# Two placement rules in a weight arena: how many places early gate loads must leave, and where output blocks go

## The chip, the cores and the metric

The kernel runs on one core of one Trainium2 chip. The time is that of the device for one launch, in microseconds, and lower is better. TensorE (PE) multiplies, VectorE (DVE), ScalarE (ACT) and GpSimd (POOL) do the rest, and every large transfer is issued from the queue of SyncE (SP).

## The reference

Eight sequences of 448 positions pass through an attention block of 12 heads (head size 64) with normalized queries and keys, and then through a gated feed-forward layer:

```python
q_n, k_n = rmsnorm(q, g_q), rmsnorm(k, g_k)
scores = scale * np.matmul(q_n, k_n.transpose(0, 1, 3, 2))
attn = exp(scores - max) / (sum + 1e-09)
x = np.matmul(attn, v)                 # then (B,H,S,D) -> (B*S, H*D) = (3584, 768)
xn = x / rms(x) * rms_g
g, val = xn @ w_gate, xn @ w_val       # 768 x 1536 each
out = (g * sigmoid(g) * val) @ w_out   # 1536 x 768
```

All data are float32 for the engines.

## The kernel before, in words

**Staging.** Attention runs over pairs of heads, six pairs to a sequence. While the pairs of sequence b + 1 are computed, the feed-forward work of sequence b is filled in between their blocks. `fill` (from L1630) takes the next feed-forward item from a list, calls it through `pe`, and afterwards lets other engines' work be issued. `pe` counts steps: `now["t"]` is the planner's clock, and everything that is to be issued "n steps later" (`after`) is put down by it. The order of instructions on every engine is thus fixed by this Python code, and engines run their instructions in that order.

**Gate and value of the second sequence (b = 1).** From the second sequence on, the two products with `w_gate` and `w_val` are made together, with a scheme of 15 products of thirds and halves of the matrices (`PRODUCTS`) in place of 18. It runs over four groups of three 128-wide column blocks, in the order 0, 2, 1, 3 (`GROUPS`), called here the first to the fourth. One product is eight matmuls of 224 columns (L1182). Its weight operand is either one of nine raw blocks (`b11` to `b33`) or one of nine sums of two or three raw blocks (`v9`, `v4`, `v5`, `v7`, `v1`, `v14`, `v11`, `v10`, `v13`, in the order of their use). The left operands are sums too, made once per sequence. What leaves PSUM is added up on VectorE (L1200, L1203, L1255) or copied by ScalarE (L1197), and a finished column block becomes `h` through L1214 and L1215.

For the second sequence alone the weight sums do not exist yet. Each is made by `derive` on VectorE: a first `tensor_tensor` of 128x512 at L1087, a second at L1090, or only one of them. It is put five steps later into a scratch tensor in HBM (`kept`, L1095), from where later sequences load it ready-made. `derive` makes the sums strictly in order, only from raw blocks whose loads were asked for five or more steps ago, and only if a place is free. `fill` calls it once a step at the third and fourth step after a block of attention has begun, and later than that up to about two instructions a step. If a product is due whose sum is missing, the sum is made at once.

**Places.** All weight blocks lie in an arena of 66 units of 128 columns (`places`, `block`, `give_back`). A gate block takes 4 units, aligned to 4 (kind `wg`; `wg1` adds six spare places outside the arena); an output block takes 3 units, counted from the upper end (kind `w`). While sums of the output weights for the third sequence are still to be made (`todo_q` is not empty), the upper 18 units are set apart (kind `side`), which leaves 48 units: 12 + 6 places for gate blocks, or 16 for output blocks, in the same units. `block` takes the place that has been free longest. A block of the second sequence is given back three steps after its last use, others one step after.

**Loads.** `ask` (L1038) runs whenever a place comes free. It goes through one list of uses: the nine raw blocks of each of the four groups, then the 42 output blocks of the second sequence, then the third sequence's gate blocks, and so on. A load is issued (L1066) only if `keep_free` places would still be free after it: 6 for the second sequence's gate blocks, 3 for others, 1 for the first seven of the third sequence. Output blocks wait until all 36 weight sums are made. Blocks for the side sums (`wd`, `wx`, L1046) go into the side zone.

**Output sums.** `derive_o` (L1122) makes sums of output-weight blocks for the second sequence, and only in steps in which `derive` made none. `derive_q` (L1150 to L1153) makes those for the third sequence, in 21 jobs of four instructions. It needs two free gate places, and it is held back while one of the third sequence's first seven gate loads is the next to be asked for. The output products of the second sequence are at L1447 and those of the third at L1518.

Of the kernel before, what the change touches and what calls it, by code (L numbers as in the profile page):

```python
# [335 lines left out]
def safe_scores(  # L336
# [40 lines left out]
    now, due = {"t": 0}, []  # L377
# [146 lines left out]
    def norm_k(g, half):  # L524

        if g >= NG:
            return
        for n in range(NK * half, NK * (half + 1)):
            block = st["qk", g][:, 1, n * D:(n + 1) * D]
            nc.scalar.activation(block, block, ACT.Copy, scale=st["rs", g][:, 2 * NK + n:2 * NK + n + 1])  # L530
# [248 lines left out]
    def hurry(jobs):  # L779
        while jobs:  # L780
# [12 lines left out]
    RIGHT_G = {"v9": ("b11", "b33", None), "v4": ("b21", None, "b32"), "v5": ("b12", None, "b23"),  # L793
               "v1": ("b21", "b33", "b31"), "v14": ("b12", "b21", "b22"), "v11": ("b22", "b23", "b32"),
               "v10": ("b13", "b12", "-b33"), "v13": ("b13", "b11", "b23"), "v7": ("b31", "b11", "-b32")}
# [41 lines left out]
    freed = {i: 0 for i in range(UNITS)}  # L837
# [11 lines left out]
    def zone():  # L849

        return 18 if todo_q else 0

    def places(kind):

        lim = UNITS - (zone() if count["done"] else 0)
        if kind[0:2] == "wg":
            spans = [range(i, i + 4) for i in range(0, lim - 3, 4)]
            if kind == "wg1":
                spans += [range(i, i + 4) for i in sorted(spare) if i % 4 == 0]
        elif kind == "side":  # L860
            spans = [range(i, i + 3) for i in range(lim, UNITS, 3)]
        else:
            spans = [range(i - 3, i) for i in range(lim, 2, -3)]
        return [span for span in spans if None not in [freed[i] for i in span]]

    def block(kind="w"):
        span = min(places(kind), key=lambda span: (max(freed[i] for i in span), span[0]))
        for i in span:
            freed[i] = None
        if span[0] in spare:  # L870
            return spare[span[0]], span
        return arena[:, span[0] * 128:span[-1] * 128 + 128], span

    def room(many, kind="w"):
        return len(places(kind)) >= many
# [11 lines left out]
    def data(key):  # L887
        return st[key][0][:, 0:GW if key[0] == "wg" else BW]
# [40 lines left out]
    turn_of, count = {"n": 0}, {"done": False, "cv": 0}  # L929
# [8 lines left out]
    def home(key):  # L938
        if key[0] == "w":
            g, j = divmod(key[2], KG)  # L940
            at = 2 * key[4] + key[3]
            return kept[g, j:9:3, :, at * 128:(at + 1) * 128].rearrange("k p n -> p k n")
        if key[0] == "wg":
            return kept[key[2], NAMES_G.index(key[3])]
        if key[0] == "wq":
            n = min(2, PARTS_Q - 2 * key[3]) * HW
            return kept_q[key[2]][:, 2 * HW * key[3]:2 * HW * key[3] + n]
        return kept_o[NAMES.index(key[2]), key[3]]
# [5 lines left out]
    def convert():  # L954
# [5 lines left out]
        if 0 <= n - 5 < len(pieces):  # L960
            key = pieces[n - 5][0]
            st[key] = block()
            lo, top = st.pop(("cv", n - 5))
            nc.gpsimd.tensor_tensor(data(key).bitcast(I32), top, lo, ALU.add)
# [61 lines left out]
    asked = {"n": 0, "derived": 0}  # L1026
# [4 lines left out]
    derived = [(g, to) for g in GROUPS for _, _, to in PRODUCTS if to in RIGHT_G]  # L1031
# [6 lines left out]
    def ask():  # L1038

        if turn_of["n"] < TURNS:  # L1040
            return
        while side and (room(1, "side") or side[0][0] == "wd" and asked["derived"] > 32 and room(4, "wg")):
            key = side.pop(0)
            asked[key] = now["t"]
            st[key] = block("side" if room(1, "side") else "wg")
            nc.sync.dma_start(out=data(key), in_=home(key))  # L1046
        while asked["n"] < len(uses):
            key = uses[asked["n"]]
            kind, keep_free = "wg" if key[0] == "wg" else "w", 3
            if key[1] == 1 and key[0] == "wg":  # L1050
                kind, keep_free = "wg1", 6
            elif asked["derived"] < len(derived):
                return
            elif asked["n"] in next_gate:
                keep_free = 1
            if key[0] == "wo" and key[2][0] == "T" and ("kept", *key[2:]) not in asked:
                return
            if key[0] == "wq" and asked.get("sums_q", 0) < KG * (key[2] + 1):
                return
            if not room(keep_free + 1, kind):  # L1060
                return
            asked["n"] += 1
            asked[key] = now["t"]
            st[key] = block(kind)
            src = home(key)
            nc.sync.dma_start(out=data(key)[:, 0:src.shape[-1]], in_=src)  # L1066
# [66 lines left out]
    todo_q = list(jobs_q)  # L1133
# [34 lines left out]
    def used(key):  # L1168
        give_back(key)
        after(3 if key[0:2] == ("wg", 1) else 1, ask)  # L1170
# [459 lines left out]
    def fill(n=None):  # L1630
# [8 lines left out]
        for _ in range(min(n, len(todo))):  # L1639
# [5 lines left out]
            while asked["derived"] < made or (key and key not in st):  # L1645
                before = dict(asked)
                derive(0)
                if key and key[0] == "wo":
                    derive_o(0)
                ask()  # L1650
                if before == asked:
                    pe(idle)
# [263 lines left out]
```

## Time and profile before

| what | us |
|---|---|
| three runs: lowest, median, highest | 1530.95, 1531.31, 1538.87 |
| the profiled execution, its own time | 1533.21 |
| the profiled execution, first to last instruction (span) | 1531.4 |
| TensorE busy in the span | 1484.1 |
| VectorE, GpSimd, ScalarE busy | 1039.9, 738.6, 604.0 |

A row of the groups or of a timeline names the engine, the line of the code, the operation, the tile written and the tiles read, and how often it ran; a bracket at its end gives the idle time just before it and what ended it. "raw", "top" and "top_x" are names of spare tiles that serve as weight places or left operands; "w" is the arena. A row of the waits names the waiting instruction and the one that it waited for, with the total, the count and the longest. A row of the stretches gives, after the stretch and its length, the busy time of each engine, the clock granted to TensorE (1.00 is full), the busy share of the DMA engines and GB/s. The second sequence's gate and value stage lies between 285 and about 424 us of the span, its output stage from there to 490, and the third sequence's two stages from 490 to about 680.

### The profile page before, as it was taken

Reading aid. Unit: us, or ns where it says so; the run is one execution under the profiler, and the core shown is the slowest. Engines: PE = TensorE matmul, PEld = TensorE weight load, DVE = VectorE, ACT = ScalarE, POOL = GpSimd, SP = SyncE. Lnnn points to the kernel's source line nnn. Section 1 sums busy time; section 2 is a strip of 40 time slices with the busy share of each in tenths; the row PEclk is TensorE's granted clock in tenths of the full one; section 3 lists DMA queues with packets and bytes.
Section 4 is the critical chain, followed back from the end, with each engine's and each line's share of the span. In section 5 each row is a group of like instructions: output and inputs, shape, how many; then the busy total and the mean of one; then the engine's idle time right before and its main releaser. Section 6 shows DMA issues by size and latency. Waiting matters only on the chain.

```text
span 1531.4 us, 25718 instructions
## 1 busy us (share of the span) xinstructions
PE 1484.1 (97%) x8732; PEld 1155.8 (75%) x8732; DVE 1039.9 (68%) x1826; ACT 604.0 (39%) x1377; POOL 738.6 (48%) x708
## 2 busy tenths in 40 slices
PE   8999999998999999899999999999999999999997
PEld 4344445687755888787988788759788789899996
DVE  5777999687855687874568655635668655674664
ACT  6856765344322443224442443334542443201100
POOL 6967987555433453364544644345644632021002
PEclk9999999999999999999999999999999999999998
DMA  7758675775577899885557865576457755597675
GB/s 190 224 164 237 183 237 169 231 250 187 188 235 231 283 309 317 285 254 191 174 152 237 247 186 160 162 228 190 133 162 246 223 157 145 154 301 227 167 237 170
DMA packets 302176, 322.51 MB, mean 211 GB/s; under 512 B 81620, under 2 KB 243668, under 8 KB 302036
## 3 DMA queue, kind: packets, MB, share of 16 engines
q1 hardware_dynamic: 301108, 320.58, 68.8%
q8 instruction: 72, 1.18, 0.3%
q14 instruction: 68, 0.56, 0.1%
q10 hardware_dynamic: 800, 0.20, 0.1%
q0 software_dynamic: 128, 0.00, 0.0%
HBM read 266.90 MB, written 53.77 MB: 209 GB/s over the span
## 4 chain that ended last, share of the span: by engine, by line
PE 83%; DVE 10%; DMA 2%; issue 2%; SPq 1%; ACT 1%; POOL 1%; DVEq 0%; POOLq 0%; ACTq 0%
PE ff L1182 37%; PE ff L1518 12%; PE sc L659 8%; PE av L674 7%; PE ff L1589 6%; PE ff L1447 5%; PE tr L545 2%; PE ff L1320 1%; PE den L692 1%; DVE l L1392 1%; PE den L607 1%; PE sc L563 1%; DMA vt<-in_v_dram 1%; PE av L590 1%; DVE ms L496 1%
## 5 line engine op out<-in xcount | busy, mean ns | idle before, releaser
L714 POOL TENSOR_TENSOR es<-es,e 128x448 f32<-128x448 f32 x205 | 252.2, 1230 | 13.6
L1182 PE MATMUL ff<-x,w 128*128 128x224 f32 x1272 | 254.0, 353 | 1.4 <-DVE pb L1203 1.1
L1182 PEld LDWEIGHTS ff<-x,w 128*128 128x128 f32 x1272 | 238.5, 190 | 4.2 <-DVE pb L1203 1.4
L659 PE MATMUL sc<-qT,kT 64*64 64x448 f32 x1176 | 232.7, 541 | 5.6 <-DVE x L744 3.9
L674 PE MATMUL av<-e,vt 64*64 64x448 f32 x984 | 193.3, 538 | 0.0
L664 ACT ACTIVATE e<-sc 128x448 f32<-128x448 f32 x294 | 155.0, 547 | 80.9 <-PE sc L659 59.4
L1182 PE MATMUL ff<-xs,w 128*128 128x224 f32 x848 | 168.4, 353 | 2.6 <-DVE w L1087 1.3
L1182 PEld LDWEIGHTS ff<-xs,w 128*128 128x128 f32 x848 | 158.6, 190 | 6.3 <-issue 3.4
L644 POOL TENSOR_TENSOR ss<-ss,rd 128x448 f32<-128x448 f32 x40 | 46.8, 1170 | 210.3 <-ACT rd L643 210.3
L659 PEld LDWEIGHTS sc<-qT,kT 64*64 64x64 f32 x1176 | 78.8, 133 | 88.2 <-issue 59.9
L709 POOL TENSOR_TENSOR es<-e 128x448 f32<-128x448 f32 x41 | 47.3, 1154 | 192.5 <-ACT e L664 192.5
L1518 PE MATMUL ff<-w,l 128*128 128x192 f32 x630 | 119.1, 331 | 6.8 <-DVE pb L1552 3.0
L1203 DVE TENSOR_TENSOR pc<-ff,l 128x448 f32<-128x448 f32 x56 | 34.9, 623 | 122.9 <-PE ff L1182 91.7
L515 POOL TENSOR_TENSOR rs<-ms,mhalf 128x12 f32<-128x12 f32 (+1 forms) x50 | 115.3, 2307 | 4.2
L1518 PEld LDWEIGHTS ff<-w,l 128*128 128x128 f32 x630 | 104.2, 191 | 13.8 <-DVE pb L1552 4.2
L1589 PE MATMUL ff<-x,w 128*128 128x448 f32 x288 | 111.8, 541 | 0.0
L674 PEld LDWEIGHTS av<-e,vt 64*64 64x64 f32 x984 | 66.0, 133 | 41.3 <-issue 41.3
L1200 DVE TENSOR_TENSOR pb<-ff,pb 128x448 f32<-128x448 f32 x84 | 52.4, 623 | 63.0 <-PE ff L1182 53.5
L1589 PEld LDWEIGHTS ff<-x,w 128*128 128x128 f32 x288 | 53.3, 190 | 51.1 <-issue 47.6
L1182 PE MATMUL ff<-top_x,w 128*128 128x224 f32 x424 | 89.4, 361 | 2.1 <-DVE w L1090 2.1
L1182 PEld LDWEIGHTS ff<-top_x,w 128*128 128x128 f32 x424 | 80.2, 193 | 13.4 <-issue 10.2
L1489 POOL TENSOR_TENSOR y<-y,pa 128x384 f32<-128x384 f32 x10 | 11.3, 1154 | 157.4 <-DVE y L1564 144.4
(210 smaller groups left out, 2892.2 us busy)
## 6 DMA issues: line engine op xcount, KB each, us to landing
w<-kept SPq DMA_DIRECT2D x383, 256.0 KB, 3.4
w<-kept_q SPq DMA_DIRECT2D x350, 192.0 KB, 3.8
w<-kept_o SPq DMA_DIRECT2D x150, 192.0 KB, 4.0
kept_q<-w SPq DMA_DIRECT2D x63, 192.0 KB, 3.4
qk<-in_q_dram SPq DMA_DIRECT2D x48, 192.0 KB, 3.8
qk<-in_k_dram SPq DMA_DIRECT2D x96, 96.0 KB, 3.8
raw<-in_moe_w_gate_dram SPq DMA_DIRECT2D x24, 384.0 KB, 4.5
raw<-in_moe_w_val_dram SPq DMA_DIRECT2D x24, 384.0 KB, 4.3
```

Source lines behind the costliest of these rows:

```text
L515: nc.gpsimd.tensor_tensor(st["rs", g][:, cols], ms, mhalf[:, cols], ALU.pow)
L644: after(m, lambda: (nc.gpsimd.tensor_tensor(ss, ss, rd, ALU.add), st.update({("summed", b): hp})))
L659: nc.tensor.matmul(ps[r, 0:S], lhsT=st["kT", g][r, keys_of(i)], rhs=st["qT", g][r, :], start=True, stop=True)
L664: nc.scalar.activation(e, ps[:, 0:S], ACT.Exp)
L674: nc.tensor.matmul(st["av", g][own(j), 0:S], lhsT=vt, rhs=st["e", g, i][r], start=i == 0, stop=i == PARTS - 1, skip_group_check=True)
L709: nc.gpsimd.tensor_tensor(st["es", g], st["e", g, 0], st["e", g, 1], ALU.add)
L714: nc.gpsimd.tensor_tensor(st["es", g], st["es", g], st["e", g, i], ALU.add)
L1182: nc.tensor.matmul(bank[:, w * HT:(w + 1) * HT], lhsT=data(key)[:, (2 * w + c) * 128:(2 * w + c + 1) * 128], rhs=a[left][:, c, :], start=o ...
L1200: nc.vector.tensor_tensor(T[name], ps[:, 0:S], T[name], ALU.add)
L1447: nc.tensor.matmul(ps, lhsT=left_o(b, which, LEFT_O[name], c), rhs=data(("wo", b, name, c)), start=first and c == 0, stop=c == NFP - 1, sk ...
L1518: nc.tensor.matmul(ps, lhsT=a[:, j, :], rhs=data(key)[:, n % 2 * HW:(n % 2 + 1) * HW], start=start and j == 0, stop=j == KG - 1, skip_grou ...
L1589: nc.tensor.matmul(bank[w][:, 0:S], lhsT=data(key)[:, c * 128:(c + 1) * 128], rhs=st["x", 0][:, 3 * half + c, :], start=half == c == 0, st ...
```

## The change

It touches two functions. In `ask`, the raw gate blocks of the second sequence must leave six places free only until the first group's nine sums are made; from then on four are enough. In `block`, an output block that is placed while the side zone exists takes, among the places that have been out of use for at least two steps, the highest one, and otherwise the longest-free one, the highest first; it used to take the place that was free longest, the lowest first.

```diff
     def block(kind="w"):
-        span = min(places(kind), key=lambda span: (max(freed[i] for i in span), span[0]))
+        last = lambda span: max(freed[i] for i in span)
+        order = lambda span: (last(span), span[0])
+        if kind == "w" and count["done"] and todo_q:
+            order = lambda span: (max(last(span), now["t"] - 2), -span[0])
+        span = min(places(kind), key=order)
@@ in ask()
             if key[1] == 1 and key[0] == "wg":
-                kind, keep_free = "wg1", 6
+                kind, keep_free = "wg1", 4 if asked["derived"] >= len(RIGHT_G) else 6
```

`RIGHT_G` holds the nine sums, and `asked["derived"]` counts the sums made so far over all groups. No instruction is added or removed by either edit.

## The prediction

> **What bounds the kernel now.** I read the page first. TensorE is busy in 1484.1 of 1531.4 us, so all its idle time together is 47.3 us, and an edit that moves loads and removes no work can win only a part of that.
>
> ```profile
> PE 1484.1 (97%) x8732; PEld 1155.8 (75%) x8732; DVE 1039.9 (68%) x1826; ACT 604.0 (39%) x1377; POOL 738.6 (48%) x708
> ```
>
> Then I cut the span into the stages that the edits reach. Columns: stretch, length, busy PE, PEld, DVE, ACT, POOL, clock, DMA share, GB/s.
>
> ```profile
> 285.00:435.00 150.00, 136.99 (x814) 111.12 (x816) 128.32 (x203) 56.58 (x133) 72.05 (x64) 0.99 0.66 216
> 435.00:490.00 55.00, 55.00 (x259) 30.42 (x252) 23.52 (x46) 18.04 (x44) 24.27 (x23) 1.00 0.76 232
> 490.00:580.00 90.00, 89.66 (x555) 75.64 (x554) 66.09 (x130) 37.14 (x84) 40.80 (x40) 1.00 0.91 289
> 580.00:690.00 110.00, 102.60 (x670) 87.63 (x670) 88.34 (x164) 35.18 (x84) 52.56 (x47) 0.98 0.90 283
> 345.00:350.00 5.00, 3.08 (x17) 2.47 (x15) 4.93 (x6) 4.03 (x12) 4.83 (x4) 1.00 0.67 226
> 360.00:365.00 5.00, 2.99 (x10) 2.81 (x11) 4.35 (x7) 0.66 (x2) 2.47 (x2) 0.77 0.87 270
> 630.00:635.00 5.00, 2.54 (x11) 1.14 (x12) 2.38 (x4) 0.67 (x2) 1.13 (x2) 0.73 0.55 161
> ```
>
> The second sequence's gate stage leaves PE idle for 13.0 us (150 - 136.99) with DVE at 86%; its output stage leaves none; the third sequence's stages leave 7.7 us, nearly all after 580, with DMA at 0.9. The waits of PE from 285 to 430 say on whom:
>
> ```profile
> PE ff L1182 <- DVE pb L1200: 2.8, 2, 2.4
> PE ff L1182 <- DVE raw L1090: 2.7, 3, 1.3
> PE ff L1182 <- DVE w L1090: 2.1, 1, 2.1
> PE ff L1447 <- DMA w<-kept_o: 2.0, 1, 2.0
> PE ff L1182 <- DVE w L1087: 1.3, 1, 1.3
> ```
>
> L1087 and L1090 are the weight sums, made just before their products; L1200 queues behind them on DVE. The timelines of PE and of DVE show one place:
>
> ```profile
> 347.60 1.75 PE L1182 MATMUL ff<-x,raw 128*128 128x224 f32 x8 [1.27 <-DVE raw L1090]
> 350.59 1.78 PE L1182 MATMUL ff<-raw 128*128 128x224 f32 x8 [1.24 <-DVE raw L1090]
> 354.75 1.75 PE L1182 MATMUL ff<-xs,w 128*128 128x224 f32 x8 [0.87 <-PE ff L1182]
> 362.01 4.95 PE L1182 MATMUL ff<-top_x,w 128*128 128x224 f32 x16 [2.15 <-DVE w L1090]
> ```
>
> ```profile
> 322.32 0.69 DVE L1090 TENSOR_TENSOR w<-w 128x512 f32<-128x512 f32 x1
> 345.95 1.50 DVE L1090 TENSOR_TENSOR raw<-raw,w 128x512 f32<-128x512 f32 x1
> 349.03 1.50 DVE L1090 TENSOR_TENSOR raw<-raw,w 128x512 f32<-128x512 f32 x1
> ```
>
> The sixteen matmuls at 362.01 took 4.95 us; elsewhere sixteen take 3.19.
>
> [...] POOL is busy for 4.83 of the 5 us around the slow ones[...]. [...] The trace shows 0.77 after single waits of no more than 2.15 us[...].
>
> **The change part by part.** No instruction is added or removed; only the steps at which loads and sums are issued change. I counted free places through the planner's code, in its steps (about 1.5 us for a product).
>
> *Four places instead of six.* Before, the second group's last raw blocks b22 and b13 are asked for at steps 187 and 190, since only then a seventh place is free. With four, the ninth sum of the first group is made at step 172 and the fifth place comes free at 174: b11, b21, b23 go at 174, b31 and b22 at 175, b13 at 176. Carrying the count on (sum in order, five steps after its load, one place each):
>
> - second group: sums v14, v11, v10, v13 at 185, 186, 187, 189 (before: 192, 193, 200, 201; v10 and v13 are used at 203, 204);
> - third group: loads from 190 to 203 (before 192 to 204), all sums by 209 (before 222);
> - fourth group: sums from 219 to 231 (before 228 to 242);
> - first output block asked for at about 235 (before 243), all of `B11` well ahead of its use from 250 (before, its last block was asked for at 250, the very step).
>
> The lowest count of free places on the way is one, so no sum is refused.
>
> Costs and gains, in order of time:
>
> 1. New: four sums of two instructions fall between steps 185 and 189. 8 x 0.69 = 5.5 us of DVE, less 2.6 us of L1122 that steps aside, are 2.9 us in front of the addition which frees the bank for product q0. In the trace that addition (L1203 at 330.48) ended 0.7 us before q0 began, so PE waits 2.2; I take 2.3. Bounds: 0 and 5. What is late next is nothing: a block of attention (5.7 us of PE with little DVE) follows.
> 2. The place at 347 to 362: waits of 1.27 + 1.24 + 0.87 + 2.15 = 5.53, and 4.95 - 3.19 = 1.76 by the clock, 7.29 in all. The sums of v10 and v13 (0.97 + 1.50 + 1.02 + 1.50 = 5.0 us of DVE) are gone from here, but v4, v5 and v7 come in front of the last addition of the group: 4 more instructions, about 2.8 us. That addition, which the second product of the next group waits for, ended at 355.8 less the latency; it ends about 2 us sooner, and PE, which reaches it 2.5 us sooner, waits 2.6 us there. Gain 7.29 - 2.6 = 4.7. Bounds: 1 and 7.3.
> 3. 0.37 at 385.84 and 1.30 at 393.83 (v9 of the fourth group, made two steps before use, now eleven): 1.3 of 1.67. Bounds: -1 and 1.7.
> 4. 0.22 at 414.51 and 2.44 at 421.75: the fourth group's last four sums (8.3 us of DVE from 408 to 418) are made nine or more steps earlier; and 1.99 at 429.15 for the output block. 4.65, of which I take 4.3. Bounds: 2 and 4.65.
>
> *Highest place.* Before, the scattered output blocks leave one or two gate places (none to two right after loads) from step 253 to 284 though 9 units are free. `derive_q` needs two: of its 21 jobs two run before 290, the last at step 379. Its four instructions ran at 627.73 to 631.8 on DVE, three of them at 1.28 us, and in front of the L744 that PE's scores waited 3.86 us for. Packed to the upper end, the nine free units hold two gate places more often. I count one to three more jobs before 280, each later one sooner by as many turns of the side zone. From 580 to 690 the waits are 0.42 + 1.45 + 3.86 + 1.00 + 0.67 = 7.4 and the clock some 1.3 (0.73 in 630 to 635): 8.7. I take 2.4, since DMA stays at 0.9 and the output sums at L1392 stay. Bounds: -3 and 8.7. The 55.00 of 55.00 in the output stage mean that nothing can be won there.
>
> Sum: -2.3 + 4.7 + 1.3 + 4.3 + 2.4 = 10.4 us. The profiled execution took 1533.21, 1.8 us more than its span and 1.9 above the median; the gain goes off both: 1522.8 for it, 1521 for the median of 1531.31.
>
> **Rivals.**
>
> *The waits only move.* DVE works through the same 60 sum instructions (22.84 + 27.41 us in this stage). If POOL's contention hits the bunched ones, items 1 and 2 cancel and only items 3 and 4 remain, at some 4 us, with no gain later: 1527.5, within the bound. For it: 86% DVE load, and 1.50 us for 0.69. Against it: DVE was idle for half of 340 to 345 and of 365 to 380, and the first group's nine sums, bunched in the same way, cost PE only 1.08 us.
>
> *More is won.* All waits of items 2 to 4 and those after 580 go, item 1 is nil: 7.3 + 1.7 + 4.65 + 5 = 18.6, 1513.
>
> *The output blocks come late (slower).* Where `derive_q` gets its two places sooner, it holds up to 8 of the 9 free units for four steps, and the next output blocks, which must leave three places, are asked for late. Six blocks serve a sum of four steps (5.9 us); landing takes a median of 4.1 us, so it decides once a block is asked for less than three steps ahead. Seven names at two late loads of 1.2 us each are 17 us, less the 8 of items 1 to 4: 1540. For it: PE already waited 1.99 us for such a block. Against it: jobs are at least three steps apart, each gives its places back after four, and the stage has no wait today.
>
> That the change does nothing can't be: the fifth place is free at 174.
>
> **How the numbers follow.** Forecast 0.58 (1515 to 1525 for itself), waits only move 0.18, more is won 0.11, slower 0.13. The likeliest is 1521. Leaving out half of the slower case and half of the best, the range is 1513.5 to 1533. A difference of 0.5%, 7.7 us, is about what a measurement tells from none: faster means below 1523.7. Nine tenths of the forecast and all of the best case lie there: 0.63. Within the 0.5% lie the rest of the forecast, the moved waits and a little of the slower case: 0.25. Slower: 0.12.
>
> **What would show it.** Right: no PE wait on L1087 or L1090 after 330; none on kept_o near 425; the four sums of the second group's end before 335; `derive_q` instructions ended before 625 and no 3.9 us wait for L744. Item 1 shows as a wait for L1203 near 332, item 2 as one of 2 to 3 us near 351. Wrong: PE waits on L1200, L1203 or L1255 that add up to 8 us or more from 320 to 370, or waits of L1447 on kept_o between 430 and 490.

## The result, and the profile after

The changed kernel takes 1528.84 us in the median of 11 runs (1525.72 to 1531.57), the kernel before, run beside it, 1532.77 (1529.15 to 1538.87). The ratio is 0.9972, 95% interval 0.996 to 0.9984: a gain of some 4 us where 10.4 were forecast, and short of the 1523.7 us that the prediction called faster.

The profiled execution took 1528.56 us, its span 1526.8. In the busy row of the page, TensorE's work is what it was, so the 4.6 us that the span lost are idle time of TensorE.

```profile
PE 1484.6 (97%) x8732; PEld 1156.9 (76%) x8732; DVE 1037.8 (68%) x1826; ACT 602.9 (39%) x1377; POOL 738.6 (48%) x708
```

The stretches of the changed kernel, with the columns of the table in the prediction (stretch, length, busy PE, PEld, DVE, ACT, POOL, clock, DMA share, GB/s), and a short one behind a wait:

```profile
285.00:435.00 150.00, 139.56 (x834) 112.31 (x836) 131.99 (x206) 57.50 (x135) 73.77 (x65) 0.98 0.72 230
435.00:490.00 55.00, 55.00 (x245) 30.76 (x238) 22.19 (x44) 16.54 (x42) 23.24 (x23) 1.00 0.69 204
490.00:580.00 90.00, 89.67 (x560) 76.46 (x559) 65.43 (x129) 37.65 (x85) 40.78 (x40) 1.00 0.92 292
580.00:690.00 110.00, 104.53 (x693) 88.56 (x695) 85.77 (x163) 37.01 (x88) 53.47 (x48) 0.98 0.91 285
335.00:340.00 5.00, 5.00 (x28) 2.75 (x32) 4.15 (x8) 0.85 (x2) 0.00 (x0) 0.66 0.88 263
```

The gate stage still leaves PE idle for 10.4 us (150 - 139.56; 13.0 before), and its clock is lower (0.98 for 0.99). The wait for L744 near 630 is down from 3.86 to 1.26 us, and the scores behind it run at full clock (1.00 from 630 to 635, 0.73 before). First the kernel before, then the changed one:

```profile
632.46 1.01 PE L659 MATMUL sc<-qT,kT 64*64 64x448 f32 x2 [3.86 <-DVE x L744]
```

```profile
629.95 0.59 PE L659 MATMUL sc<-qT,kT 64*64 64x448 f32 x2 [1.26 <-DVE x L744]
```

The four longest waits of PE in the gate stage of the changed kernel (total, count, longest):

```profile
PE ff L1186 <- DVE pc L1207: 2.9, 1, 2.9
PE ff L1186 <- DVE pb L1204: 2.4, 1, 2.4
PE ff L1451 <- DMA w<-kept_o: 2.1, 2, 1.7
PE ff L1186 <- issue: 1.6, 1, 1.6
```

All line numbers are four higher than before, so L1207 is the old L1203 and L1451 the old L1447. No wait on a weight sum (now L1091 and L1094) is left. What took their place is seen in PE's timeline:

```profile
334.83 2.51 PE L1186 MATMUL ff<-l,w 128*128 128x224 f32 x8 [2.90 <-DVE pc L1207]
337.27 1.77 PE L692 MATMUL den<-es,ones 64*64 64x448 f32 x8
...
357.27 1.75 PE L1186 MATMUL ff<-xs,w 128*128 128x224 f32 x8 [1.62 <-issue]
...
417.96 3.29 PE L1186 MATMUL ff<-raw,w 128*128 128x224 f32 x8 [2.39 <-DVE pb L1204]
...
425.27 1.56 PE L1451 MATMUL ff<-w,top 128*128 128x384 f32 x4 [1.68 <-DMA w<-kept_o]
427.25 0.91 PE L1451 MATMUL ff<-w,top 128*128 128x384 f32 x2 [0.43 <-DMA w<-kept_o]
```

Eight of these matmuls take 1.78 us at full clock; behind the 2.90 and the 2.39 they took 2.51 and 3.29. The granted clock was 0.50 from 336 to 339 and from 418 to 421: this is what is called half clock below.

A second trace of each kernel (two of the experiments) tells what belongs to the kernel and what to the execution. The stages below run from one block of attention on PE to another, named by where the blocks begin in the kernel before. Two values are the two traces; the change is between their means.

| stage | forecast | before | after | change |
|---|---|---|---|---|
| 306 to 334 (item 1) | +2.3 | 28.38, 28.38 | 33.02, 33.14 | +4.7 |
| 334 to 368 (item 2) | -4.7 | 34.20, 32.51 | 28.63, 28.52 | -4.8 |
| 368 to 398 (item 3) | -1.3 | 29.43, 29.42 | 27.14, 27.14 | -2.3 |
| 398 to 434 (item 4) | -4.3 | 36.03, 35.93 | 37.37, 39.70 | +2.6 |
| 434 to 661 (item 5) | -2.4 | 227.51, 228.07 | 225.35, 225.77 | -2.2 |
| sum | -10.4 | | | -2.0 |

After 661 another 0.9 us is gained. The spans of the two traces differ by 2.95 us in the mean, the medians by 3.9; what half clock cost in one trace of a kernel and not in the other, 1.7 us (4.95 for 3.27) and 1.5 us (3.29 for 1.78), is of this size. Items 2 and 5 came as forecast, and item 3 gave 1.0 more. Item 1 cost twice its price. Item 4 turned from a gain of 4.3 into a loss of 2.6, which alone is 6.9 of the 8.4 that these stages fell short by.

### The profile page after: what moved, and what is told of

Its sections match the earlier page's. It is cut to its first block, busy times and chain, and to the rows that moved or that the text cites. A ratio compares the mean times of both kernels' runs of the same rounds, so it can differ in the third digit from the quotient of the medians.

```text
span 1526.8 us, 25696 instructions
## 1 busy us (share of the span) xinstructions
PE 1484.6 (97%) x8732; PEld 1156.9 (76%) x8732; DVE 1037.8 (68%) x1826; ACT 602.9 (39%) x1377; POOL 738.6 (48%) x708
## 4 chain that ended last, share of the span: by engine, by line
PE 81%; DVE 11%; DMA 3%; issue 2%; SPq 2%; ACT 1%; POOL 1%; DVEq 0%; POOLq 0%; ACTq 0%
PE ff L1186 38%; PE ff L1522 11%; PE sc L659 7%; PE av L674 7%; PE ff L1451 5%; PE ff L1593 5%; PE ff L1324 2%; PE tr L545 2%; DVE l L1396 1%; PE den L692 1%; PE den L607 1%; PE sc L563 1%; PE av L590 1%; DVE ms L496 1%; DVE top L919 1%
## 5 line engine op out<-in xcount | busy, mean ns | idle before, releaser
L1186 PE MATMUL ff<-x,w 128*128 128x224 f32 x1304 | 260.9, 353 | 1.4 <-DVE pb L1207 1.1
L714 POOL TENSOR_TENSOR es<-es,e 128x448 f32<-128x448 f32 x205 | 252.7, 1233 | 13.6
L1186 PEld LDWEIGHTS ff<-x,w 128*128 128x128 f32 x1304 | 244.1, 190 | 5.2 <-DVE pb L1207 1.4
L1186 PE MATMUL ff<-xs,w 128*128 128x224 f32 x832 | 164.8, 353 | 1.6 <-issue 1.6
L1207 DVE TENSOR_TENSOR pc<-ff,l 128x448 f32<-128x448 f32 x56 | 34.9, 623 | 119.4 <-PE ff L1186 78.4
L1593 PEld LDWEIGHTS ff<-x,w 128*128 128x128 f32 x288 | 53.3, 190 | 51.1 <-issue 47.6
L1186 PE MATMUL ff<-l,w 128*128 128x224 f32 x408 | 82.8, 355 | 2.9 <-DVE pc L1207 2.9
```

The costliest lines, as they stand in the source:

```text
L714: nc.gpsimd.tensor_tensor(st["es", g], st["es", g], st["e", g, i], ALU.add)
L1186: nc.tensor.matmul(bank[:, w * HT:(w + 1) * HT], lhsT=data(key)[:, (2 * w + c) * 128:(2 * w + c + 1) * 128], rhs=a[left][:, c, :], start=o ...
L1593: nc.tensor.matmul(bank[w][:, 0:S], lhsT=data(key)[:, c * 128:(c + 1) * 128], rhs=st["x", 0][:, 3 * half + c, :], start=half == c == 0, st ...
```

## The experiments

**The second edit alone.** The kernel before with the new order in `block` and the old `keep_free` of 6.

> Only the second edit (output blocks take the highest place); the gate loads still leave six places. Theory (the first edit does all the work in the second sequence's gate stage, the second edit only moves the third sequence's output sums): from 285 to 424 us everything as before, PE waits of 1.27 + 1.24 + 0.87 + 2.15 near 350 and 2.4 near 420; the last sum for the third sequence is issued one planner step sooner than before (378 for 379), so of the 2.7 us that the changed kernel gained after 435 at most 1 is left: ratio 0.9993 to 1.000. Rival (the gain after 435 belongs to the place rule): the wait for L744 near 630 is 1.3 us as in the changed kernel, and the ratio is 0.998.

Measured: 1529.7 us against 1533.59, ratio 0.9971 (0.9959 to 0.9984), the ratio of the whole change. The waits in the gate stage are those of before. In the third sequence the wait for L744 is gone, and the two blocks of attention that lie near 592 and 661 in the kernel before are 65.99 us apart, where that kernel has 69.64. In this one trace a new wait before that, and the half clock behind it (granted clock 0.67 from 585 to 590), cost all of it again (the stage from 434 to 661 takes 227.50 us, as in the kernel before):

```profile
585.99 4.95 PE L1186 MATMUL ff<-xs,w 128*128 128x224 f32 x16 [2.40 <-DMA w<-kept]
```

So over eight executions the placement rule is worth what the whole change is worth, to within some 3 us by the two intervals, and the first edit on top of it adds nothing that shows: by the table, items 1 to 4 sum to +0.2. Where the placement rule alone has its gain, this one trace does not show. The first edit alone has no run: with the old placement, blocks of the third sequence's last set of output weights have not been asked for when their product is due.

**The sums of the second group spread.** The changed kernel, in which a sum of the second group is made at most five products ahead of its use.

```diff
@@ in derive()
+        due_at = GROUPS.index(g) * len(PRODUCTS) + [right for _, _, right in PRODUCTS].index(to)
+        if wait and len(RIGHT_G) <= asked["derived"] < 2 * len(RIGHT_G) and due_at - asked.get("products", 0) >= 6:
+            return False
@@ in product()
+        if b == 1:
+            asked["products"] = asked.get("products", 0) + 1
```

> The changed kernel, but a sum of the second group may be made at most five products ahead of its use, so that v14, v11, v10, v13 are issued at steps 189, 190, 192, 193 and not at 185 to 189. Theory (item 1 is the bunch of eight sum instructions in front of the addition that frees the bank of q0): the wait of 2.90 us near 332 falls below 0.5, the half clock after it is gone, and the block of attention that began at 337.3 begins at 333.4 to 334.2; the rest of the changed kernel's gain stays. The planner also asks for the last block of B11 two steps before use, so the kept_o waits (2.1 us) fall below 1. Ratio to before 0.9945 (1524.3). Rival (DVE is simply full in this stage and the wait only moves): PE waits as much in 345 to 370 as is won near 332, and the ratio stays at 0.997.

Measured: 1524.37 us, ratio 0.9938 (0.9925 to 0.9952), better than the change. PE's timeline:

```profile
331.53 1.78 PE L1191 MATMUL ff<-l,w 128*128 128x224 f32 x8 [1.03 <-DVE pc L1212]
352.59 1.75 PE L1191 MATMUL ff<-xs,raw 128*128 128x224 f32 x8 [1.87 <-issue]
413.28 1.99 PE L1191 MATMUL ff<-raw,w 128*128 128x224 f32 x8 [2.39 <-DVE pb L1209]
422.10 1.56 PE L1456 MATMUL ff<-w,top 128*128 128x384 f32 x4 [2.38 <-DMA w<-kept_o]
```

The wait of 2.90 is 1.03 and the clock behind it full (1.00 from 330 to 340): the first stage takes 29.68 us for 33.02, and the second keeps its gain (28.72). The bunching of sums was item 1's cost, and it was not needed for item 2. It is not all that this run gained over the changed kernel: the stages from 434 to 661 take 222.30 us for 225.35 and 225.77, with the last job of `derive_q` at step 374 in place of 376. The waits on `kept_o` were expected to fall below 1 us and did not (2.38), though the last block is now asked for at step 248, two steps before its use.

**Without the late output sums.** The changed kernel without the VectorE instructions of `derive_o` for the column blocks 4 and 5 (L1126; their part of the output is not computed).

```diff
-        nc.vector.tensor_tensor(data(key), a, b, ALU.subtract)
+        if c < 4:
+            nc.vector.tensor_tensor(data(key), a, b, ALU.subtract)
```

> The changed kernel without the last eight instructions of L1126 (output-weight sums of the last two columns are left out, so the second sequence's output differs); loads, stores and all steps stay. They take 4.97 us of DVE between 411.6 and 419.0. Theory (the wait of 2.39 us at 417.96 stayed because these sums were issued five steps sooner, in front of the addition that frees the last product's bank): the wait falls below 0.4 and the half clock there is gone, so the output stage begins 3 to 3.9 us sooner relative to the block at 393.8. Rival (v10 and v13 of the fourth group, 5.3 us at 405 to 411, are what is late): the wait stays at 1.5 or more.

Measured: 1520.36 us in one execution. The wait of 2.39 us and its half clock are gone. The stage from 398 to 434 takes 33.24 us for 37.37, though PE still waits 1.89 and 0.44 us on `kept_o` in it. VectorE's timeline of the changed kernel shows why:

```profile
409.69 1.51 DVE L1094 TENSOR_TENSOR w<-w,raw 128x512 f32<-128x512 f32 x1
411.12 0.61 DVE L1204 TENSOR_TENSOR pb<-ff,pb 128x448 f32<-128x448 f32 x1
411.65 1.55 DVE L1126 TENSOR_TENSOR w<-w 128x384 f32<-128x384 f32 x2
413.12 0.62 DVE L1204 TENSOR_TENSOR pa<-ff,pa 128x448 f32<-128x448 f32 x1
413.65 1.14 DVE L1126 TENSOR_TENSOR w<-w 128x384 f32<-128x384 f32 x2
...
416.23 1.14 DVE L1126 TENSOR_TENSOR w<-w 128x384 f32<-128x384 f32 x2
417.29 0.62 DVE L1204 TENSOR_TENSOR pb<-ff,pb 128x448 f32<-128x448 f32 x1
```

Six output sums, 3.83 us, run between the last weight sum and the addition that PE waits for at 417.96. In the kernel before only two of them were in front of it, and weight sums before these:

```profile
417.89 0.69 DVE L1090 TENSOR_TENSOR w<-w 128x512 f32<-128x512 f32 x1
...
420.02 1.14 DVE L1122 TENSOR_TENSOR w<-w 128x384 f32<-128x384 f32 x2
421.08 0.62 DVE L1200 TENSOR_TENSOR pb<-ff,pb 128x448 f32<-128x448 f32 x1
```

The first edit took the weight sums away, and `derive_o`, which runs only in steps without one, moved into their place.

**Without GpSimd's additions.** The changed kernel without the additions into `es` after the first (L714) in the six pairs of heads that cover the gate stage (the softmax sums of these pairs are then not computed).

```diff
-            for i in parts:
+            for i in () if 13 <= g <= 18 else parts:
```

> The changed kernel without GpSimd's additions of exponentials after the first one (L714) in head pairs 13 to 18, so that the softmax sums of these pairs are wrong; nothing else changes. Theory (DVE instructions with two SBUF inputs took 1.2 to 1.5 us for 0.69 where GpSimd read SBUF at the same time): in 285 to 435 the mean of L1091 and L1094 falls from 0.84 to about 0.70, DVE loses 8 to 10 us of busy time, and the PE waits of that stretch (10.4 us) fall by at least half. Rival (the slow ones have another cause, such as DMA traffic on the same tiles): their mean stays above 0.8.

Measured: 1522.24 us in one execution. The stretch of the gate stage:

```profile
285.00:435.00 150.00, 142.52 (x864) 113.80 (x863) 121.34 (x206) 60.26 (x139) 47.05 (x45) 0.98 0.71 230
```

VectorE ran 206 instructions in the stretch in both kernels, in 121.34 us for 131.99. The 60 weight sums alone took 43.40 for 48.05. In the changed kernel's own trace, L714 runs on GpSimd from 405.98 to 412.19; beside it the second instructions of two sums (L1094 at 406.60 and 409.69) took 1.51 us each for 0.69, while the additions between them that read PSUM (408.03, 411.12) took 0.61. The waits of 1.62 and 2.39 are gone, so GpSimd's additions lengthen what stands in front of the products of items 2 and 4. PE's idle time fell from 10.4 to 7.5 us, less than the half that was expected; a wait on `kept_o` took 3.12 us in this execution. The 2.89 near 332 stays. This does not clear GpSimd there: L520 and L469 are left in this kernel, and in the trace of the changed kernel two of the eight bunched sum instructions, each beside one of them, took 1.00 and 1.20 us for 0.69. Without this excess of 0.8 us the wait would be some 2.1 us, an estimate from these durations: most of it is the bunch itself.

**Output blocks asked for earlier.** The changed kernel, in which the first six output blocks leave one place, not three. The planner then asks for five of them at step 240 and the last at 248, where the changed kernel asks at 240, 248 and 250.

```diff
             elif asked["n"] in next_gate:
                 keep_free = 1
+            elif key[0] == "wo" and key[1] == 1 and asked["n"] < 4 * 9 + 6:
+                keep_free = 1
```

> The changed kernel, in which the first six output blocks (B11) need leave only one place free, not three. Counted through the planner: five of them are asked for at step 240 and the last at 248, where the changed kernel asks at 240, 248 and 250 (the step of use); the jobs of derive_q are the same to within two steps. If the waits on kept_o (1.68 and 0.43 us in the changed kernel) come from the rule of three places, as I hold, they fall to under 0.5 us in all and the time is some 1.6 us below the changed kernel's, a ratio of about 0.996 to the kernel before. Rival: the transfers that start at 240 compete with the side loads and the stores of the sums, and the block still lands late: waits on kept_o of 1.5 us or more, and the time of the changed kernel.

Measured: 1524.14 us against 1533.62, ratio 0.9942 (0.9925 to 0.9958): some 4.7 us below the changed kernel, not 1.6.

```profile
417.41 3.28 PE L1188 MATMUL ff<-raw,w 128*128 128x224 f32 x8 [2.39 <-DVE pb L1206]
424.65 0.91 PE L1453 MATMUL ff<-w,top 128*128 128x384 f32 x2 [0.16 <-DMA w<-kept_o]
```

The stage from 398 to 434 takes 35.33 us, where the changed kernel took 37.37 and 39.70. The other half of the gain was not expected: the stages from 434 to 661 take 222.47 us for 225.35 and 225.77. The last job of `derive_q` is at step 374 instead of 376, the wait for L744 is gone, and PE waits 1.50 us near 609 where the changed kernel waits 2.55 and 2.84 near 612.

**The two kernels once more.** No edit.

> The kernel before once more, for a second trace. The gate stage's waits should be the same to 0.1 us (1.27, 1.24, 0.87, 2.15; 0.37, 1.30; 0.22, 2.44; 1.99 on kept_o). If the half clock after the 2.15 us wait (sixteen matmuls in 4.95 us for 3.19) is bound to that wait, it is there again; if it is an accident of the execution, the sixteen take 3.2 to 3.4 us and the stage is about 1.7 us shorter. The wait of 1.99 on kept_o was 0.38 with the placement rule alone: if that is the doing of the rule, it is 1.9 to 2.1 here.

```profile
360.36 3.27 PE L1182 MATMUL ff<-top_x,w 128*128 128x224 f32 x16 [2.14 <-DVE w L1090]
418.39 3.31 PE L1182 MATMUL ff<-raw,w 128*128 128x224 f32 x8 [2.43 <-DVE pb L1200]
425.71 0.91 PE L1447 MATMUL ff<-w,top 128*128 128x384 f32 x2 [0.38 <-DMA w<-kept_o]
```

> The changed kernel once more, for a second trace. Waits the same to 0.1 us: 1.08, 2.90, 1.62, 0.34, 2.39, and on kept_o 1.68 and 0.43, if they follow from the order of work; a wait on kept_o that differs by 0.5 us or more is one of the transfers' spread. The stretch between the blocks of attention near 306 and 334, which was 33.02 us against 28.38 before, should be 33.0 again if 2.9 us of wait and 1.7 us of half clock are both bound to the place, and 31.3 if the half clock is an accident.

```profile
333.21 2.65 PE L1186 MATMUL ff<-l,w 128*128 128x224 f32 x8 [2.89 <-DVE pc L1207]
416.36 1.78 PE L1186 MATMUL ff<-raw,w 128*128 128x224 f32 x8 [2.39 <-DVE pb L1204]
423.92 4.21 PE L1451 MATMUL ff<-w,top 128*128 128x384 f32 x6 [3.44 <-DMA w<-kept_o]
```

Times 1530.6 and 1529.28, spans 1528.8 and 1527.5. In the gate stage, waits on an engine repeat to 0.03 us. Waits on a transfer do not: the 1.99 on `kept_o` of the kernel before is 0.38 here, and the 2.1 of the changed kernel is 3.44. The 0.38 of the run with the second edit alone is therefore no doing of that edit. The half clock doesn't repeat either: the sixteen matmuls that took 4.95 us take 3.27 behind the same wait (granted clock from 360 to 365: 0.77 and 1.00), and the eight of the changed kernel take 1.78 for 3.29 (1.00 from 416 to 421, 0.69 from 418 to 423 in the first trace). Behind the 2.90 near 332 they are slow both times (0.66 over 5 us in each), and so are the eight behind the 2.55 and 2.84 us near 612 (3.29 and 3.04 us).

**All three mends.** The changed kernel with the two edits above (spread sums, early output blocks) and one more:

```diff
@@ in derive_o()
+        if wait and c == 5 and asked.get("products", 0) < 60:
+            return
```

> The changed kernel with three limits more: sums of the second group at most five products ahead (as in the run that spread them), the first six output blocks leaving one place (as in the run beside this one), and the output sums of column block 5 held back until the 60th product of the gate stage is done. If the losses of the changed kernel are the three that I named (2.9 us near 332, 2.4 us at the last products of the fourth group with the clock after it, 2.1 to 2.4 us on kept_o), the stretch of the gate stage has no wait over 1.9 us left, the waits on kept_o are under 0.5, that of the last products is under 1.0, and the time is 3 to 5 us below the run with spread sums alone: 1519.5 to 1521.5, ratio 0.990 to 0.992. Rival: the last job of derive_q goes from step 374 to 395 and a wait for L744 of about 4 us comes back in the third sequence's output stage, which eats the gain: 1523 to 1525.

Measured: 1522.83 us, ratio 0.993 (0.9916 to 0.9944), about 2 us above what was expected.

```profile
413.60 1.78 PE L1195 MATMUL ff<-raw,w 128*128 128x224 f32 x8 [1.33 <-DVE pb L1213]
...
611.10 1.21 PE L1531 MATMUL ff<-w,h 128*128 128x192 f32 x6 [0.88 <-DMA w<-kept_q]
614.87 1.07 PE L1531 MATMUL ff<-w,l 128*128 128x192 f32 x4 [2.23 <-DMA w<-kept_q]
```

The stage from 398 to 434 is down to 32.16 us, with no wait on `kept_o`. But with the output sums held back only one job of `derive_q`, not two, runs before step 289. The later ones come one turn later, the last at step 395, and the third sequence waits for blocks that they make. The rival was right about the jobs, though the price fell on `kept_q` and not on L744.

**Two mends, and two mends with the sums on GpSimd.** The first has the spread sums and the early output blocks alone; the second lets GpSimd make the output sums of column block 5:

```diff
-        nc.vector.tensor_tensor(data(key), a, b, ALU.subtract)
+        (nc.gpsimd if c == 5 else nc.vector).tensor_tensor(data(key), a, b, ALU.subtract)
```

> The changed kernel with two limits more: sums of the second group at most five products ahead, and the first six output blocks leaving one place (the last one asked for at step 245). No output sum is held back, so that the jobs of derive_q stay at steps 263 to 374 as with spread sums alone, where holding back moved the last one to 395. Expected: no wait on kept_o over 0.3 us, the wait of 2.4 us at the last products of the fourth group still there, no wait on kept_q over 0.6 us in the third sequence (0.88 and 2.23 with all three), and 1520.5 to 1522.5 us, ratio 0.991 to 0.993. If the late jobs of derive_q were not what cost the run with all three its gain, this one is 2 to 3 us slower than it: 1525.

> The kernel beside it, in which GpSimd in place of VectorE makes the four output sums of column block 5 (128x384 each). The jobs of derive_q stay where they are. If the output sums in VectorE's queue are what the last products of the fourth group wait for, the wait of 2.4 us falls to under 0.9 us, the stretch between the blocks of attention near 390 and 425 gets 1.5 to 4 us shorter, and the time is 1518 to 1521. Rival: GpSimd's sums (a 128x448 addition takes it about 1.27 us) contend with VectorE and delay what GpSimd gives to the next block of attention; then the wait stays above 1.5 us or another of the same size comes up before 460, and the time is that of the kernel beside it.

Measured beside a kernel before of 1533.25: 1520.72 us, ratio 0.9914 (0.9898 to 0.9931), and 1517.9 us, ratio 0.9898 (0.9885 to 0.991). With the two mends PE has no wait on `kept_o` or `kept_q`, and the 2.39 is still there, all as expected. With the sums on GpSimd, PE's timeline and GpSimd's show:

```profile
413.72 1.78 PE L1193 MATMUL ff<-raw,w 128*128 128x224 f32 x8 [1.33 <-DVE pb L1211]
```

```profile
416.71 5.12 POOL L1131 TENSOR_TENSOR w<-w 128x384 f32<-128x384 f32 x4
425.96 2.06 POOL L709 TENSOR_TENSOR es<-e 128x448 f32<-128x448 f32 x1 [4.12 <-ACT e L664]
```

The wait is 1.33, not under 0.9. The sums of column block 4 are still on VectorE, and without both blocks' sums the wait was gone. The stage from 398 to 434 is 2.7 us shorter (34.91 to 32.17); 1.1 of this is half clock behind the 2.39 in the trace of the first version (2.88 us for 1.78). GpSimd makes the four sums in 5.12 us and then is idle for 4.12 us, so they delay nothing of its own. Behind them PE waits 0.18 us for VectorE's L744, at 426.24. This version is about 15 us faster than the kernel before and, by the ratios, 11 faster than the changed one.

**One job of `derive_q` taken out.** The kernel before without the four VectorE instructions of the last job, and the changed kernel without those of the last but one ((6, 1); the output blocks of those jobs are then not computed; loads and stores stay).

```diff
+        if (i, j) != (6, 2):
             nc.vector.tensor_tensor(tb[:, 1], x[:, 1], x[:, 0], ALU.subtract)
...
```

> The kernel before without the four VectorE instructions of the last of the 21 jobs of derive_q; its loads and stores stay. (The output blocks of that job are then not the sums.) If those four instructions (627.73 to 631.8 us, 4.07 us) are what the last L744 and with it the scores wait for, the wait of 3.86 us for L744 falls to under 0.8 us and the time between the blocks of attention near 591 and 661 is 3 to 5 us shorter than its 69.7 us. Rival: L744 waits for what comes before it in any case (the sums of squares, GpSimd), and 3 us or more of the wait stay.

> The changed kernel without the four VectorE instructions of the last but one job of derive_q; its loads and stores stay. (The output blocks of that job are then not the sums.) In the two traces of the changed kernel the first of the four waits 1.04 and 1.34 us for a store to kept_q, with VectorE's queue behind it, and 2 us later TensorE waits 2.55 and 2.84 us for an addition L1204, where the kernel before has 1.45. If the job is the cause, this wait falls to 1.0 us or less and the wait for L744 (1.26) may go as well; if not, it stays at 2.5 or more.

The first of these rows is of the kernel before without the job, the second of the changed kernel without it:

```profile
628.58 0.59 PE L659 MATMUL sc<-qT,kT 64*64 64x448 f32 x2 [0.59 <-DVE x L744]
```

```profile
610.03 1.78 PE L1187 MATMUL ff<-raw,w 128*128 128x224 f32 x8 [0.20 <-DVE pb L1205]
```

In the first, the wait of 3.86 us is 0.59, and the time between the blocks near 592 and 661 is 65.89 us for 69.64. In the second, the wait of 2.55 (2.84 in the second trace; 1.45 in the kernel before) is 0.20, that for L744 is gone, and the same time is 63.86 for 68.11 and 68.58. Both jobs were what PE waited for, through VectorE's queue. In the changed kernel the job itself stands still:

```profile
610.64 0.36 DVE L1154 TENSOR_TENSOR w<-w 128x192 f32<-128x192 f32 x1 [1.04 <-DMA kept_q<-w]
...
611.85 0.62 DVE L1204 TENSOR_TENSOR pb<-ff,pb 128x448 f32<-128x448 f32 x1
```

It waits 1.04 us for a store from the place that it writes to, with the additions behind it. Such a wait (0.75 and 0.15) is there in the kernel before without its last job as well, at the same job, and PE's wait behind it is 2.50 us; the two full traces of that kernel do not have it. So it may be part of the transfers' spread, and how much of it the change brings stays open.

## Why the prediction was too high

**Item 1, the bunched sums: right mechanism, size too small.** The wait came where it was put and on the instruction named, at 2.90 for 2.3 us. The addition on VectorE in the kernel before, and then VectorE's timeline of the changed kernel:

```profile
330.48 0.62 DVE L1203 TENSOR_TENSOR pc<-ff,l 128x448 f32<-128x448 f32 x1
```

```profile
327.56 0.69 DVE L1091 TENSOR_TENSOR w<-w 128x512 f32<-128x512 f32 x1
328.28 0.69 DVE L1094 TENSOR_TENSOR w<-w,raw 128x512 f32<-128x512 f32 x1
...
333.04 1.20 DVE L1094 TENSOR_TENSOR w<-w 128x512 f32<-128x512 f32 x1
334.17 0.61 DVE L1207 TENSOR_TENSOR pc<-ff,l 128x448 f32<-128x448 f32 x1
```

The addition runs at 334.17 where it ran at 330.48: 3.7 us later, not 2.9, because the eight instructions took more than 8 x 0.69 (two of them 1.00 and 1.20, each beside an instruction of GpSimd). The larger miss is the clock, which the sum left out: the eight matmuls after the wait took 2.51 us for 1.78 and the eight of `den` 1.77 where the kernel before has 0.98 (granted clock 0.50 from 336 to 339). Together item 1 cost 4.7. The prediction priced the half clock where it saw it go (item 2) and not where the new wait of 2.90 us brought it. "What is late next is nothing" was so.

**Items 2 and 3: right.** PE waits 1.62 and 0.34 us before the products near 357 and 359, where one wait of 2.6 was forecast. The gain of 4.7 measured 4.8, of which 0.8 is the half clock that only one of the two traces of before has. Item 3's bound of 1.7 was passed at 2.3; what gave the other 0.6 stays open.

**Item 4: the step that failed.** It said that the fourth group's last four sums are made nine or more steps earlier, that the 2.44 us wait goes with them, and that the output block is asked for in time. Each part fell:

- Two of the four sums came eight steps earlier, at 230 and 231. `v10` and `v13` came only two and three steps earlier, at 238 and 239. Both need the raw block `b13`, the last of the group, which was asked for at step 226, the same step as before, and a block of attention followed.
- The time that was won in VectorE's queue was filled by `derive_o`. Its eight late sums moved from steps 245 to 248 to 240 to 246, and six of them now stand in front of the addition that PE waits for. The wait stayed at 2.39 (2.44 before). The run without these sums lost it.
- The last output block was still asked for at step 250, the step of its use. Two side loads took gate places at steps 233 and 234, and the rule of three places held the last three blocks of `B11` back to 248 and 250. The waits on `kept_o`, 0.38 and 1.99 in the two traces of before, became 2.1 and 3.44. Relaxing the rule to one place took them to 0.16.

Counting the planner by hand went right for the second group (185, 186, 187, 189, as forecast) and for the third (done at 210 for 209), and wrong for the fourth, where the last three raw blocks (steps 222, 225 and 226) still had to wait for a fifth free place.

**Item 5: right size, wrong account.** 2.2 us came for 2.4. But `derive_q` runs no further job before step 280, and of the later ones only two move: the third comes one step earlier (289 for 290) and the last comes three steps earlier (376 for 379). That was enough to take the last from in front of the last L744. The run of the kernel before without this job shows that it cost 3.75 us, and the change got less of it, since the job before it, at step 371 in both kernels, holds up the additions near 612 for longer (2.55 and 2.84 us for 1.45, and half clock behind it).

**The rivals.** "The waits only move", at 1527.5, is nearest to the measured 1528.84, in good part by luck. Items 1 and 2 do cancel, but its reason, sums that are slower beside GpSimd, makes only some 0.8 us of item 1 (1.00 and 1.20 us for 0.69). It left items 3 and 4 standing with no gain later; in the runs items 3 and 4 cancel too, and what is left came after 434. What moved was the order in VectorE's queue. That the time lies inside the stated range is this same cancelling and no support for the account. Of the slower rival, the late output block is real, but at its old place before 430 and at 2 to 3.5 us; none was seen from 435 to 490, where PE is busy for 55.00 of 55.00 us as before.

## What to carry to other kernels

When work is pulled forward in an engine's queue, ask which other work is only held back by it: here six output sums (3.83 us of VectorE) moved up into the freed slots and kept the same addition waiting. A relaxed limit needs an end of its own, as late as its user allows: with the second group's sums spread over their products, the stage where the bunch had stood was 3.4 us shorter, nearly as much as the whole change won. Before a transfer's wait is counted as a gain, find the step at which its load is asked for, after the change, with everything else that takes places.

## What the runs showed of the hardware

- Behind waits of the same length the clock was halved in some traces and not in others. Behind 2.14 or 2.15 us, sixteen matmuls took 4.95 us in two traces and 3.27 in two (3.19 at full clock); behind 2.39 us, eight took 3.29 and 1.78 in two traces of one kernel; behind 1.88 us, 2.76 in one and 1.75 in others. Behind the 2.9 us near 332 they were slow in all six traces (2.51 to 3.36 for 1.78). But behind 3.05 us on `kept_o`, in the run without the job (6, 1), four matmuls took 1.56 us, as they do at full clock (1.00 from 425 to 427 in the changed kernel), and behind 3.12 us, in the run without GpSimd's additions, 2.15; so up to there no length was found that settles it. By the 4.95 and 3.27 us, one trace of a stage is good to some 1.7 us for each such wait, an estimate.
- VectorE kept to the order of its queue where something behind could have been used sooner: in the changed kernel it stood 1.04 us for a store to `kept_q` (610.64), with the addition of 611.85 behind it, for which PE waited 2.55 us. Without that job's four instructions PE waited 0.20 us.
- The wait for one and the same load moved between 0.38 and 1.99 us from one trace of the kernel before to the other, where the gate stage's waits on engines repeated to 0.03.
